# First MoE: the last 1024 tokens take layer one as seven products, and attention ends within two chunks

## The chip, the cores and the metric

The program runs on one core of a Trainium2 chip. The time is the device time of one execution in microseconds (us); the median of three runs of the kernel before is 2063.89 us (2061.16 to 2064.94).

## The reference, cut to what matters

Three stages follow each other. Attention with a window of 128 over 4 x 576 tokens, 8 heads of 64, gives x (2304 x 512). A first MoE layer with one expert gives g = relu(x w_in)^2 (2304 x 2048) and x2 = g w_out. A second one has eight experts that all tokens pass, weighted by a matrix that 16 alternating normalisations (the Sinkhorn loop) make from x2 w_gate.

```python
def _moe_ref(x, w_in, w_out):        # 2304 x 512, 512 x 2048, 2048 x 512
    h = x @ w_in
    r = np.maximum(h, 0.0)
    g = r * r
    return (g @ w_out).astype(np.float32)
```

## The kernel before, in words

Every fp32 product is made of two parts: a value is split into a high part (rounded by ScalarE, L113 or L117) and a low part (the difference, by GpSimd at L114 or VectorE at L114 and L118), and mm3 (L122 to L124) issues three matmuls: high by high, high by low, low by high.

The first MoE goes through the tokens in five chunks: 256 tokens (chunk 0, plain fp32 with narrowed weights), then four of 512 (chunks 1 to 4). In a chunk the 2048 columns of w_in go by in 16 steps f of 128. A step has layer one (gemm1, twelve matmuls of 512 columns into the PSUM tile h), the rectifier on ScalarE (L827), the square on VectorE (L830), the split of the square into gh and gl, and layer two of the step two before (moe1_tail, twelve matmuls into the four PSUM tiles acc). h has one PSUM buffer in chunks 0 to 3; in chunk 4 it takes the three banks that attention used (L822). Split weights are loaded from DRAM in each chunk (a from d_in, b from d_out); in chunk 1 they are split first (L113, L114). A chunk's result is split out of acc (moe1_finish), added up by GpSimd and stored to d_x2 (keep), and its gate logits come from gate_sums and gate_logits.

Attention is a list of small steps. part(i) is called three times in each f of chunks 0 to 3 and issues so many of them that the tokens of chunk c+1 are done when chunk c ends; put_x splits an attention output into xh and xl of its chunk. At the start of chunk 4 the attention pools are closed, load_q(0) loads the second MoE's first token operands, and x_op forms its seven sums and splits. After chunk 4 the slab of the second MoE's first unit is made (raw_w1, sums_w1, split_w1).

The second MoE uses Strassen's scheme in Winograd's form already: seven products for a 2 x 2 block product (GP lists the weight operand, the token operand and the PSUM bank). Its loops are not touched but for the banks of its unit 0.

Until the end of chunk 4 a scheduler orders each engine's instructions; from L859 on each engine runs in the order of the code. Each engine's queue is in order throughout.

Of the kernel before, what the change touches and what calls it, by code (L numbers as in the profile page):

```python
# [8 lines left out]
F32 = mybir.dt.float32  # L9
# [20 lines left out]
def attention_moe_moe2(  # L30
# [32 lines left out]
    NTT = NT // P  # L63

# [19 lines left out]
    xh, xl = [], []  # L84
# [18 lines left out]
    for c in range(3):  # L103
        new_x(xp, c)

# [315 lines left out]
    def put_x(ps, hp, t0, n):  # L421
        o = 0
        while o < n:
# [7 lines left out]
            split_ps(ps[:, o : o + w], xh[c][:, hp, at : at + w], xl[c][:, hp, at : at + w])  # L431
# [110 lines left out]

    words = {}
# [80 lines left out]
    def gate_sums(c):  # L624
        n = chunk(c)[1]
        lp, tag = (ps_at, "at") if c < NCH - 1 else (ps_mm, "mm")
# [17 lines left out]
    def gate_logits():  # L644
# [5 lines left out]
        lp = ps_at.tile([P, 512], F32, name="lp", tag="at")  # L650
# [122 lines left out]
    LAG = 2  # L773
    pending, sums = [], []
    turns = [(c, f) for c in range(NCH) for f in range(NF1)]
# [12 lines left out]
    for c in range(NCH):  # L788
        c0, n = chunk(c)
        if c == 1:  # L790
# [6 lines left out]
            xp2 = m1.enter_context(tc.tile_pool(name="xp2", bufs=1))  # L797
            for i in range(3, NCH):
                new_x(xp2, i)

        advance(needed(c0 + n))
        if c == NCH - 1:
            att.close()
            p2 = ctx.enter_context(tc.tile_pool(name="p2", bufs=1, side="right"))
            p3s = ExitStack()
            p3 = p3s.enter_context(tc.tile_pool(name="p3a", bufs=1, side="right"))
            load_q(0)
            for nm, eng in (("b11", 0), ("b21", 1), ("t1", 0), ("t2", 1), ("t3", 0), ("t4", 1), ("b22", 0)):
                x_op(nm, (nc.vector, nc.gpsimd)[eng])
        for f in range(NF1):  # L810
            now[:] = c, f
            a, bw = ahead.pop(0)
# [9 lines left out]
            hp, tag = (ps_mm, "mm") if c < NCH - 1 else (ps_at, "at")  # L822
            ph = hp.tile([P, 512], F32, name="h1", tag=tag)
# [28 lines left out]
    raw_w1(0)  # L852
    raw_w1(1)
    for x in range(2):
        sums_w1(0, x)
    for x in range(2):
        split_w1(0, x)

    ctx.enter_context(tc.manual_schedule())  # L859

# [63 lines left out]
    def g_product(n, p):  # L924
        o, b, bk = GP[p]
        first = p in (0, 1, 3)
        if first:
            gb[bk] = g_bank(f"g{bk}")
# [218 lines left out]

    moe1_tail(*pending[0])
    moe1_tail(*pending[1])
    moe1_finish(pending[1][0], pending[1][2])  # L1150
    pp = None
    for n in range(NP):
        if n == 0:
# [274 lines left out]
```

## Time and profile before

| | us |
|---|---|
| median of three runs | 2063.89 |
| span of the profiled execution (the only time that it has of its own) | 2061.8 |
| attention's start, until the first layer-one matmul of chunk 0 | 33 |
| chunk 0 with attention | 109 |
| chunks 1 to 3 with attention | 358 |
| chunk 4 | 88 |
| second MoE | 1474 |

The profile is of one execution. The page gives each engine's busy share; the window rows give the same for a stretch, with the granted clock of TensorE (1.00 is 2.4 GHz) and what the DMA engines moved; the timeline gives single instructions with start and duration. A matmul's duration overlaps with the next one's, so the time of a run of matmuls is read from their starts. A duration on VectorE or GpSimd includes the time for which the instruction was held back after its issue.

### The profile page before, as it was taken

What the parts mean: (1) busy time and instruction counts of PE and PEld (TensorE: products, weight loads), DVE (VectorE), ACT (ScalarE), POOL (GpSimd) and SP (SyncE); (2) the same over time, 40 slices, a digit from 0 to 9 for tenths busy, and PEclk for the clock granted to TensorE, in tenths of its full rate; (3) what the DMA queues carried; (4) which work ended last, traced back from release to release, by engine and by line L of the source; (5) the groups of instructions that cost most, each with busy time, mean ns of one, the idle gap of its engine ahead of it and who ended that gap; (6) DMA issues with size and microseconds to landing.
All of it is one profiled execution on the core that took longest, in us unless ns stands there. A gap on an engine that the chain in (4) does not pass through costs nothing.

```text
span 2061.8 us, 31510 instructions
## 1 busy us (share of the span) xinstructions
PE 2025.9 (98%) x10869; PEld 1854.1 (90%) x10869; DVE 1385.8 (67%) x2469; ACT 955.5 (46%) x1950; POOL 1080.9 (52%) x836
## 2 busy tenths in 40 slices
PE   7989999999999999999999999999999999999999
PEld 5767777887888899999999999999999999999999
DVE  7986755535147887777786766776676577667765
ACT  7665655434244444444444434444444444444443
POOL 4224343434358788788785444544454454445442
PEclk9999999999999999999999999999999999999999
DMA  7877877656649878887879878777786787877773
GB/s 208 280 211 252 265 221 195 193 164 204 209 159 327 295 307 319 320 310 287 313 297 343 285 254 256 259 259 256 253 273 228 260 256 260 258 256 235 270 260 106
DMA packets 290653, 523.84 MB, mean 254 GB/s; under 512 B 90416, under 2 KB 135104, under 8 KB 286400
## 3 DMA queue, kind: packets, MB, share of 16 engines
q1 hardware_dynamic: 290496, 521.85, 75.9%
q8 instruction: 87, 1.43, 0.3%
q14 instruction: 70, 0.57, 0.1%
HBM read 369.12 MB, written 152.64 MB: 253 GB/s over the span
## 4 chain that ended last, share of the span: by engine, by line
PE 69%; DVE 4%; issue 1%; ACT 1%; POOL 1%; DMA 0%; ACTq 0%; POOLq 0%; DVEq 0%
PE y L123 11%; PE y L124 11%; PE y L122 11%; PE g L122 11%; PE g L124 11%; PE g L123 11%; PE acc L122 1%; PE acc L123 1%; PE acc L124 1%; PE h L123 1%; PE h L122 1%; PE h L124 1%; DVE s L737 1%; DVE s L739 0%; DVE o L1044 0%
## 5 line engine op out<-in xcount | busy, mean ns | idle before, releaser
L1236 POOL TENSOR_TENSOR rb<-R,rb 128x768 fp32r<-128x768 f32 x95 | 214.0, 2253 | 345.3 <-ACT rb L1231 321.6
L1272 DVE TENSOR_TENSOR a<-y,a 128x384 f32<-128x384 f32 x420 | 232.4, 554 | 192.5 <-PE y L124 192.5
L1236 POOL TENSOR_TENSOR rt<-R,rt 128x768 fp32r<-128x768 f32 x121 | 230.4, 1915 | 138.5 <-ACT rt L1231 59.4
L114 POOL TENSOR_TENSOR w2a<-r,w2a 128x1024 fp32r<-128x1024 f32 x64 | 154.2, 2410 | 66.9 <-ACT w2a L113 66.9
L122 PE MATMUL g<-xt,w1o 128*128 128x384 f32 x512 | 173.8, 339 | 1.4 <-ACT u L947 1.0
L124 PE MATMUL g<-xt,w1o 128*128 128x384 f32 x512 | 172.6, 337 | 0.0
L123 PE MATMUL g<-xt,w1o 128*128 128x384 f32 x512 | 172.3, 337 | 0.0
L122 PE MATMUL y<-rt,w2o 128*128 128x384 f32 x496 | 168.1, 339 | 0.1
L123 PE MATMUL y<-rt,w2o 128*128 128x384 f32 x496 | 168.0, 339 | 0.0
L124 PE MATMUL y<-rt,w2o 128*128 128x384 f32 x496 | 167.4, 337 | 0.0
L1231 ACT ACTIVATE rt<-R 128x768 fp32r<-128x768 f32 x122 | 102.7, 842 | 134.7 <-DVE R L1217 84.0
L114 POOL TENSOR_TENSOR gl<-r,gh 128x512 fp32r<-128x512 f32 x64 | 83.0, 1297 | 155.9 <-ACT gh L113 130.9
L124 PE MATMUL y<-w2a,rl 128*128 128x512 f32 x384 | 150.1, 391 | 0.0
L123 PE MATMUL y<-w2a,rh 128*128 128x512 f32 x384 | 149.6, 390 | 0.2 <-POOL w2a L114 0.2
L122 PE MATMUL y<-w2a,rh 128*128 128x512 f32 x384 | 149.5, 389 | 0.0
L1212 DVE TENSOR_TENSOR R<-R,pb 128x768 f32<-128x768 f32 x128 | 138.5, 1083 | 5.4 <-ACT R L1338 3.9
L122 PE MATMUL y<-rb,w2o 128*128 128x384 f32 x408 | 138.3, 339 | 0.6 <-DVE a L1272 0.6
L123 PE MATMUL y<-rb,w2o 128*128 128x384 f32 x408 | 138.3, 339 | 0.0
L124 PE MATMUL y<-rb,w2o 128*128 128x384 f32 x408 | 137.6, 337 | 0.0
L122 PE MATMUL g<-xb,w1o 128*128 128x384 f32 x384 | 129.9, 338 | 0.0
L124 PE MATMUL g<-xb,w1o 128*128 128x384 f32 x384 | 129.5, 337 | 0.0
L123 PE MATMUL g<-xb,w1o 128*128 128x384 f32 x384 | 129.3, 337 | 0.0
(261 smaller groups left out, 5773.2 us busy)
## 6 DMA issues: line engine op xcount, KB each, us to landing
w1o<-d_w SPq DMA_DIRECT2D x448, 256.0 KB, 3.0
w2o<-d_w SPq DMA_DIRECT2D x218, 512.0 KB, 3.9
d_w<-w1a SPq DMA_DIRECT2D x32, 1792.0 KB, 11.6
d_w<-w2a SPq DMA_DIRECT2D x30, 1536.0 KB, 7.9
r<-in_moe_w_dram SPq DMA_DIRECT2D x64, 512.0 KB, 4.3
a<-d_in SPq DMA_DIRECT2D x48, 512.0 KB, 3.8
b<-d_out SPq DMA_DIRECT2D x48, 512.0 KB, 3.9
u<-in_moe_w_in_dram SPq DMA_DIRECT2D x16, 512.0 KB, 5.0
```

Of the source, the lines that this page charges most:

```text
L114: (eng or nc.gpsimd).tensor_sub(lo, src, raw(hi))
L122: nc.tensor.matmul(ps, lhsT=lh, rhs=rh, start=first, stop=False, **kw)
L123: nc.tensor.matmul(ps, lhsT=lh, rhs=rl, start=False, stop=False, **kw)
L124: nc.tensor.matmul(ps, lhsT=ll, rhs=rh, start=False, stop=last, **kw)
L737: nc.vector.tensor_sub(w1s[n][:, 2], w1s[n][:, 1], a11)
L1212: nc.vector.tensor_mul(r, r, pb[:, None, :].to_broadcast([P, 2, HALF]))
L1231: nc.scalar.activation(x[:, 0], R[m, f, h], AF.Copy)
L1236: eng.tensor_sub(x[:, 1], R[m, f, h], raw(x[:, 0]))
L1272: nc.vector.tensor_add(acc[dst][:, dt], ps[:, :HALF], acc[dst][:, dt])
```

## The change

Chunks 1 and 2 stay as they are. Chunks 3 and 4 (1024 tokens) become one block with two token halves t. Attention writes their x unsplit (xr, by ScalarE alone) and ends four steps before the end of chunk 2; in these four steps early_super splits the seven token operands (b11, b21, t1 to t4, b22: two quarters of K by 512 tokens each, 128x1024) and makes the first weight slab. Layer one then runs as eight units u of two steps f. A unit has seven products of six matmuls of 512 columns; its raw weights come from d_w, and the slab of the next unit is summed (super_sums) and split (super_split) beside it. The squares go to DRAM (d_g), as whole fp32. Four PSUM banks are used in turn, so that product 0 of the next unit stands between products 4 and 5. Layer two follows as 32 steps j, first the 16 of token half 0, then those of half 1; w and g are loaded five steps ahead and g is split two steps ahead. The second MoE's x_op, raw_w1, sums_w1 and split_w1 are spread over the steps of layer two. The diff's core:

```diff
+    PLAIN_CH = NCH - 2
...
     def part(i):
         c, f = now
-        if c < NCH - 1:
-            a, b = [needed(starts[x] + widths[x]) for x in (c, c + 1)]
+        if c == 0:
+            a, b = [needed(starts[x] + widths[x]) for x in (0, 1)]
             advance(a + (b - a) * (3 * f + i) // (3 * NF1))
+        else:
+            a, b = needed(starts[2]), len(steps)
+            advance(min(b, a + (b - a) * (3 * (f + (c - 1) * NF1) + i) // (3 * ((PLAIN_CH - 1) * NF1 - CALM))))
...
+    def early_super(at):
+        if at == 0:
+            advance(len(steps))
+            att.close()
+            sp = sps.enter_context(tc.tile_pool(name="sp", bufs=1, side="right"))
+            super_raw(0)
+            super_raw(1)
+            super_x("b11", 0)
+            super_x("b21", 1)
+        elif at == 1:
+            super_sums(0, False)
+            super_sums(0, True)
+            super_split(0, False)
+            super_x("t1", 0)
+        elif at == 2:
+            super_split(0, True)
+            super_x("t2", 0)
+            super_x("t3", 1)
+        else:
+            super_raw(2)
+            super_x("t4", 0)
+            super_x("b22", 1)
...
+            if c == PLAIN_CH - 1 and f >= NF1 - CALM:
+                early_super(f - NF1 + CALM)
...
-            hp, tag = (ps_mm, "mm") if c < NCH - 1 else (ps_at, "at")
-            ph = hp.tile([P, 512], F32, name="h1", tag=tag)
+            ph = ps_mm.tile([P, 512], F32, name="h1", tag="mm")
...
+    def s_evict(u, p):
+        v1, v3, v2 = s_banks(u)
+        if p == 0:
+            nc.scalar.copy(s_temp("m1"), v1)
+        elif p == 1:
+            super_split(u + 1, False)
+            nc.vector.tensor_add(v3, v3, stemps["m1"])
+            s_square(u, v3, 0, 0)
+        elif p == 2:
+            nc.scalar.copy(s_temp("u2"), v1)
+            super_sums(u + 1, False)
+        elif p == 3:
+            super_sums(u + 1, True)
+        elif p == 4:
+            nc.scalar.copy(s_temp("u3"), v1)
+            super_split(u + 1, True)
+            nc.vector.tensor_add(v3, v2, stemps["u3"])
+            s_square(u, v3, 1, 1)
+        elif p == 5:
+            super_raw(u + 3)
+            s_square(u, v1, 1, 0)
+        elif p == 6:
+            nc.vector.tensor_add(v2, v2, stemps["u2"])
+            s_square(u, v2, 0, 1)
...
+    slots = [(0, 0)]
+    for u in range(NU):
+        slots += [(u, 1), (u, 2), (u, 3), (u, 4), (u + 1, 0), (u, 5), (u, 6)]
+    moe1_tail(*pending[0])
+    for u, p in slots:
+        if u == NU:
+            b_product(0, (0, 1))
+            b_load(4)
+            continue
+        s_product(u, p)
+        if (u, p) == (0, 0):
+            moe1_tail(*pending[1])
+        s_evict(u, p)
...
+    X_AT = {4: ("b11", 0), 5: ("b21", 1), 6: ("t1", 0), 7: ("t2", 1), 8: ("t3", 0), 9: ("t4", 1), 10: ("b22", 0)}
+    for j in range(2 * NF1):
+        if j:
+            b_product(j, range(NK))
+        b_load(j + 5)
+        b_split(j + 2)
+        if j in X_AT:
+            nm, eng = X_AT[j]
+            x_op(nm, (nc.vector, nc.gpsimd)[eng])
```

In super_x and x_op, t1 to t4 each begin with a subtraction on VectorE in place; the number behind the name says which engine makes the low part, 0 for VectorE and 1 for GpSimd.

**The burst of splits on VectorE.** Before, at the start of chunk 4: q are the second MoE's token quarters, xb and xt its operands, h_5995 the layer-one result of f = 0, acc the finished chunk 3.

```order
L830 SCALAR_TENSOR_TENSOR r<-h_5959,r 128x512
L114 TENSOR_TENSOR xb_5930<-q,xb_5930 128x768
L703 TENSOR_TENSOR q<-q 128x768
L707 TENSOR_TENSOR q<-q 128x768
L114 TENSOR_TENSOR xt_5937<-q,xt_5937 128x768
L114 TENSOR_TENSOR xb_5952<-q,xb_5952 128x768
L705 TENSOR_TENSOR q<-q 128x768
L114 TENSOR_TENSOR xt_5945<-q,xt_5945 128x768
L709 TENSOR_TENSOR q<-q 128x768
L830 SCALAR_TENSOR_TENSOR r<-h_5995,r 128x512
L118 TENSOR_TENSOR xl_2008<-acc_5081,xh_2007 128x512
```

With the change, in the last four steps of chunk 2: xr are the unsplit token quarters, sb and st the operands (5147 is b11, 5198 t1), ss the weight sums, h_5157 and h_5205 the results of f = 12 and 13.

```order
L118 TENSOR_TENSOR sb_5147<-xr_2015,sb_5147 128x1024
L810 TENSOR_TENSOR xr_2015<-xr_2016,xr_2015 128x1024
L917 SCALAR_TENSOR_TENSOR r<-h_5157,r 128x512
L839 TENSOR_TENSOR ss<-sr 128x256
L843 TENSOR_TENSOR ss<-sr 128x256
L840 TENSOR_TENSOR ss<-ss,sr 128x256
L814 TENSOR_TENSOR xr_2016<-xr_2016 128x1024
L842 TENSOR_TENSOR ss<-sr,ss 128x256
L118 TENSOR_TENSOR st_5198<-xr_2015,st_5198 128x1024
L812 TENSOR_TENSOR xr_2015<-xr_2016,xr_2015 128x1024
L917 SCALAR_TENSOR_TENSOR r<-h_5205,r 128x512
L816 TENSOR_TENSOR xr_2015<-xr_2015 128x1024
```

A burst of the same kind moves from chunk 4 into chunk 2, with pieces of 1024 columns for 768, and squares stand inside it. On GpSimd the same place reads, before and with the change:

```order
L114 TENSOR_TENSOR gl<-r,gh 128x512
L114 TENSOR_TENSOR xb_5933<-q,xb_5933 128x768
L114 TENSOR_TENSOR xt_5941<-q,xt_5941 128x768
L114 TENSOR_TENSOR xt_5949<-q,xt_5949 128x768
L114 TENSOR_TENSOR gl<-r,gh 128x512
```

```order
L118 TENSOR_TENSOR sb_5150<-xr_2015,sb_5150 128x1024
L118 TENSOR_TENSOR sb_5291<-xr_2016,sb_5291 128x1024
L118 TENSOR_TENSOR sw<-sr,sw 128x6x128
L118 TENSOR_TENSOR gl<-r,gh 128x512
L118 TENSOR_TENSOR st_5244<-xr_2016,st_5244 128x1024
L118 TENSOR_TENSOR sw<-ss,sw 128x8x128
```

Three splits of 768 become five of 768 to 1024 (sb_5150 is b21, sb_5291 b22, st_5244 t3, sw the slab).

**TensorE at the next layer-one product.** Before, in chunk 4, from layer two of the step before into layer one of f = 1, with what each waits for in brackets:

```order
L122 MATMUL acc_5093<-gh,b 128x512
L123 MATMUL acc_5093<-gl,b 128x512
L124 MATMUL acc_5093<-gh,b 128x512
L122 MATMUL h_6039<-xh_2009,a 128x512 [waits DMAHW0_49,PE_49]
L123 MATMUL h_6039<-xl_2010,a 128x512
```

With the change, in chunk 2, into layer one of f = 13:

```order
L126 MATMUL acc_4148<-gh,b 128x512
L127 MATMUL acc_4148<-gl,b 128x512
L128 MATMUL acc_4148<-gh,b 128x512
L126 MATMUL h_5205<-xh_93,a 128x512 [waits DMAHW6_49,DVE_49]
L127 MATMUL h_5205<-xl_94,a 128x512
```

The first matmul of h waits for VectorE here, since the square of the step before reads the same bank.

**VectorE through one unit.** In chunk 4 of before VectorE had one square for each step and nothing else; with the change a unit reads as follows (s1 to s3 are the PSUM banks, sm1, su2 and su3 ScalarE's copies, gs the squares, ss the sums for the next unit):

```order
L979 TENSOR_TENSOR s1_5333<-s1_5333,sm1_5891 128x512
L970 SCALAR_TENSOR_TENSOR gs_5928<-s1_5333,r_5926 128x512
L839 TENSOR_TENSOR ss_5939<-sr_5814 128x256
L840 TENSOR_TENSOR ss_5939<-ss_5939,sr_5814 128x256
L842 TENSOR_TENSOR ss_5939<-sr_5814,ss_5939 128x256
L843 TENSOR_TENSOR ss_5939<-sr_5814 128x256
L989 TENSOR_TENSOR s1_5333<-s2_5334,su3_5956 128x512
L970 SCALAR_TENSOR_TENSOR gs_5963<-s1_5333,r_5961 128x512
L970 SCALAR_TENSOR_TENSOR gs_5986<-s0_5332,r_5984 128x512
L995 TENSOR_TENSOR s2_5334<-s2_5334,su2_5937 128x512
L970 SCALAR_TENSOR_TENSOR gs_5998<-s2_5334,r_5996 128x512
```

Two squares of a pair of steps become four squares, three additions and four sums for 42 layer-one matmuls.

## Rows read from the trace of the kernel before

**Rows 1.** The page, busy us of each engine (share of the span) x instructions.
```profile
PE 2025.9 (98%) x10869; PEld 1854.1 (90%) x10869; DVE 1385.8 (67%) x2469; ACT 955.5 (46%) x1950; POOL 1080.9 (52%) x836
```
**Rows 2.** Timeline of PE in chunk 4: start, duration (us), line, names, shapes.
```profile
560.78 0.39 PE L122 MATMUL h<-xh,a 128*128 128x512 f32 x1
...
563.50 0.39 PE L122 MATMUL acc<-gh,b 128*128 128x512 f32 x1
...
579.59 0.39 PE L124 MATMUL h<-xh,a 128*128 128x512 f32 x1
```
**Rows 3.** Windows of chunk 0: length, busy us (x count), clock, DMA share, GB/s.
```profile
33.00:142.00 109.00, 103.49 (x561) 80.14 (x560) 99.63 (x285) 73.33 (x217) 22.09 (x38) 0.98 0.81 245
```
**Rows 4.** Windows of chunks 1 to 3 (PE, PEld, DVE, ACT, POOL).
```profile
142.00:202.00 60.00, 57.44 (x306) 44.56 (x306) 41.76 (x129) 37.27 (x101) 27.05 (x45) 1.00 0.75 245
202.00:262.00 60.00, 58.35 (x312) 45.68 (x310) 41.06 (x130) 38.32 (x106) 21.25 (x33) 1.00 0.84 270
262.00:382.00 120.00, 119.40 (x653) 95.14 (x652) 66.34 (x237) 61.36 (x182) 44.84 (x76) 1.00 0.72 202
382.00:500.00 118.00, 117.88 (x592) 94.34 (x591) 46.73 (x135) 45.26 (x113) 40.79 (x57) 1.00 0.60 187
```
**Rows 5.** Timeline of PE where chunk 4 begins, idle before in brackets.
```profile
502.27 0.39 PE L629 MATMUL lt<-xh,wgs 128*72 128x512 f32 x1
504.95 0.50 PE L122 MATMUL acc<-gh,b 128*128 128x512 f32 x1 [2.29 <-DVE xl L118]
505.29 0.40 PE L123 MATMUL acc<-gl,b 128*128 128x512 f32 x1
...
507.44 0.63 PE L123 MATMUL acc<-gl,b 128*128 128x512 f32 x1
507.87 0.63 PE L124 MATMUL acc<-gh,b 128*128 128x512 f32 x1
```
**Rows 6.** Windows where chunk 4 begins and in the second MoE.
```profile
502.00:510.00 8.00, 5.71 (x18) 4.01 (x18) 8.00 (x10) 4.70 (x9) 7.01 (x5) 0.79 0.31 108
800.00:850.00 50.00, 50.00 (x252) 45.33 (x251) 38.18 (x55) 23.68 (x39) 42.60 (x33) 1.00 0.92 355
```
**Rows 7.** Timeline of DVE: subtractions, a square, sums of the second MoE.
```profile
496.86 2.50 DVE L707 TENSOR_TENSOR q<-q 128x768 f32<-128x768 f32 x1
...
501.01 0.94 DVE L705 TENSOR_TENSOR q<-q 128x768 f32<-128x768 f32 x1
...
580.71 0.69 DVE L830 SCALAR_TENSOR_TENSOR r<-h,r 128x512 f32<-128x512 f32 x1 [4.75 <-ACT r L827]
...
621.72 0.42 DVE L736 TENSOR_TENSOR s<-r 128x256 f32<-128x256 f32 x1
622.17 2.51 DVE L737 TENSOR_TENSOR s<-s,r 128x256 f32<-128x256 f32 x1
```
**Rows 8.** Timeline of POOL beside them.
```profile
495.97 2.57 POOL L114 TENSOR_TENSOR xb<-q,xb 128x768 fp32r<-128x768 f32 x1
...
507.13 1.30 POOL L114 TENSOR_TENSOR gl<-r,gh 128x512 fp32r<-128x512 f32 x1
...
613.00 2.41 POOL L114 TENSOR_TENSOR w1a<-s,w1a 128x1024 fp32r<-128x1024 f32 x1
...
621.83 2.56 POOL L114 TENSOR_TENSOR w2a<-r,w2a 128x1024 fp32r<-128x1024 f32 x1 [1.17 <-ACT w2a L113]
```
**Rows 9.** Timeline of ACT: a split of 1024 and a rectifier.
```profile
512.48 1.06 ACT L113 ACTIVATE w1a<-s 128x1024 fp32r<-128x1024 f32 x1 [4.53 <-DVE s L739]
...
580.08 0.60 ACT L827 ACTIVATE r<-h 128x512 f32<-128x512 f32 x1 [3.45 <-PE h L124]
```

More of the change, by code (lines that the diff above doesn't have):

```diff
@@ L82, in chunk @@
         return starts[c], widths[c]
-    xh, xl = [], []
+    xh, xl, xr = [], [], []
     def new_x(pool, c):
@@ L541, in narrow @@
         nc.vector.tensor_add(w, t[2], t[3])
+    d_g = [dram.tile([P, 2, 2, CH], F32, name=f"d_g{u}") for u in range(NF1 // 2)]
     words = {}
@@ L787, in attention_moe_moe2, with super_x @@
     qstack = []
-    for c in range(NCH):
+    xr_stack = ExitStack()
+    sps = ExitStack()
+    sx, sr, ss, sslab = {}, {}, {}, {}
+    NU = NF1 // 2
+    def super_x(nm, eng):
+        q = {(h, t): xr[t][:, 2 * h : 2 * h + 2] for h in range(2) for t in range(2)}
+        if nm == "t1":
+            nc.vector.tensor_sub(q[0, 0], q[0, 1], q[0, 0])
+        elif nm == "t2":
+            nc.vector.tensor_sub(q[0, 0], q[1, 1], q[0, 0])
+        elif nm == "t3":
+            nc.vector.tensor_sub(q[0, 1], q[1, 1], q[0, 1])
+        elif nm == "t4":
+            nc.vector.tensor_sub(q[1, 0], q[1, 0], q[0, 0])
+        at = {"b11": (0, 0), "t1": (0, 0), "t2": (0, 0), "b21": (1, 0), "t4": (1, 0), "t3": (0, 1), "b22": (1, 1)}[nm]
+        x = sx[nm] = sp.tile([P, 2, 2, CH], F32R, name=f"s{nm}")
+        split_sb(q[at], x[:, 0], x[:, 1], (nc.vector, nc.gpsimd)[eng])
@@ L789, in attention_moe_moe2 @@
+    sp = None
+    for c in range(PLAIN_CH):
         c0, n = chunk(c)
@@ L796, in attention_moe_moe2 @@
                     nc.gpsimd.memset(raw(x), 0.0)
-            xp2 = m1.enter_context(tc.tile_pool(name="xp2", bufs=1))
-            for i in range(3, NCH):
-                new_x(xp2, i)
+            xp2 = xr_stack.enter_context(tc.tile_pool(name="xp2", bufs=1))
+            for i in range(PLAIN_CH, NCH):
+                xr.append(xp2.tile([P, NK, CH], F32, name=f"xr{i}"))
         advance(needed(c0 + n))
[L802 to L809, printed above, removed]
         for f in range(NF1):
             now[:] = c, f
+            if c == PLAIN_CH - 1 and f >= NF1 - CALM:
+                early_super(f - NF1 + CALM)
             a, bw = ahead.pop(0)
@@ new lines, in attention_moe_moe2, with b_product @@
+    baccs = []
+    def b_product(j, ds):
+        h, f = divmod(j, NF1)
+        (w, _), (gh, gl) = btiles[j], bparts[j]
+        for d in ds:
+            if f == 0 and h == 0:
+                baccs.append(ps_acc.tile([P, 512], F32, name=f"acc{d}", tag="acc"))
+            acc1 = sbank[d] if h else baccs[d]
+            col = slice(d * P, (d + 1) * P)
+            mm3(acc1, (w[:, 0, col], w[:, 1, col]), (gh, gl), f == 0, f == NF1 - 1)
+            if f == NF1 - 1:
+                finish_part(PLAIN_CH + h, d, acc1)
```

143 lines of the change are left out of this document (128 added, 15 removed).

## The prediction

> **What bounds the kernel now.** I read the page first, then busy time by stage, then what TensorE waited for, then the timelines of the stages that the change touches. TensorE is busy 98% of the span [rows 1], so a change pays by taking matmuls away, and it costs whatever TensorE then has to wait. A 512-column matmul of the first MoE starts every 0.227 us: twelve of them lie between 560.78 and 563.50 [rows 2]. The window rows give what the other engines let through by stage. In chunk 0 TensorE is idle 5.5 of 109 us with VectorE 91% busy [rows 3]. In chunks 1 to 3 it is idle 2.6 of 60 us at a VectorE share of 70%, 1.7 of 60 at 68%, 0.6 of 120 at 55%, 0.1 of 118 at 40% [rows 4]. Where chunk 4 begins there is one hole of some size: a matmul starts at 502.27, the next at 504.95, and then the matmuls are 0.43 us apart, at the lower of the two clock levels (1.2 GHz) [rows 5]. Between 502 and 510 only 18 start, where 35 fit, at a granted clock of 0.79 [rows 6]: 17 x 0.227 = 3.9 us lost.
>
> **What the change takes away.** Layer one of chunks 3 and 4 took 2 x 16 x 12 = 384 matmuls of 512 columns. Seven products of six matmuls for eight units are 336. 48 x 0.227 = **-10.9 us**. Layer two keeps its 384. The hole at the start of chunk 4 came from the second MoE's operand splits, put there together with the end of chunk 3. They now stand one to a step of layer two, so I take the whole hole off: **-4.0 us**.
>
> **The new burst ahead of the Strassen products.** In the last four steps of chunk 2 (f = 12 to 15) VectorE gets, beside its four squares, four subtractions and four low parts of 1024 columns and four sums of 256. GpSimd gets three low parts of 1024, the first slab's 768 and 1024, and the usual low parts of g. What this costs hangs on how the two engines stand each other. A 768-column subtraction on VectorE takes 0.94 us alone (501.01), and 2.50 us (496.86 to 499.36) beside a GpSimd split that ran from 495.97 to 498.54. A 256-column sum takes 0.42 alone (621.72), and 2.51 (622.17 to 624.68) beside a split that ended at 624.39 [rows 7, 8]. In both, VectorE's end is GpSimd's end plus a rest under 1 us: the instructions go one after the other, and by turns where both have work queued. The Trainium skill, SBUF — State Buffer, section "Who interferes with whom", states this as a rule that speaks against the change: a VectorE instruction with two SBUF inputs and a GpSimd instruction that reads SBUF share a port pair, and the one that comes later is blocked until the other is done. The two pairs of rows agree with it. The rows could also be read as two engines that share a rate (0.94 stretched to 2.50, 2.41 to 3.3); worked through in that way, the holes below come to 10 us, by the rule to the 11.6 of the hand schedule, and the bounds hold both.
>
> Why that reaches TensorE: in chunk 2 the layer-one result h has one PSUM buffer, so the matmuls of f+1 wait until VectorE has squared f, and between the two stand only twelve layer-two matmuls, 2.72 us. In chunk 4 of before h had three buffers. VectorE's queue is in order, and between the square of 12 and that of 13 stand seven instructions of the burst.
>
> By hand, from the first matmul of h(12), t = 0: ScalarE copies the last attention tile and makes three high parts of 1.06 [rows 9] before the rectifier of 12, done at 4.5. VectorE: low part b11 1.85 to 3.1 (1024 columns alone: 0.94 and 0.42 give 1.04 ns a column, so 1.21). GpSimd: low part b21 (2.41 [rows 8]) 3.1 to 5.5. VectorE: t1 5.5 to 6.7, square of 12 to 7.4. h(13) could have started at 5.44 and starts at 7.45: **2.0 us**. Then by turns: GpSimd b22 to 9.05, a sum to 9.5, GpSimd slab 768 (1.8: 2.57 less its wait, 495.97) to 11.3, a sum, GpSimd g(12) (1.3) to 13.0, a sum to 13.4, t3 to 14.6, the last sum to 15.05, low t1 to 16.3, GpSimd t3 to 18.65, t2 to 19.9, square of 13 to 20.6. h(14) was due at 7.45 + 5.44 = 12.9 and starts at 20.65: **7.75**. Then t4, low t2 and low t4, between GpSimd's slab sums and g(13), to 27.2, square of 14 to 27.9: h(15) due at 26.1, starts at 27.95: **1.85**. Sum 11.6. Ends: if nothing takes turns, VectorE's work between two squares is 4 x 0.42 + 3 x 1.21 + 0.69 = 6.0 against 5.44, a stall of about 1; if turns fall worse, 15. The idle of 2.3 us at 502 was followed by a stretch at 1.2 GHz that cost eight matmuls 0.2 us each, 1.6 us [rows 5]; here most of such a stretch falls into time that h(15) waits anyway, so I add 0.8 (0 to 3.2, two such stretches). **+12.4 us**, 1 to 18.
>
> **The Strassen products.** Each unit has one tight loop. From the end of product 6 of the unit before: result visible (579.59 + 0.23 to 580.08, so 0.27 [rows 2, 9]), VectorE's add 0.69, rectifier 0.60, square 0.69 (580.71 [rows 7]), the next add 0.69, rectifier 0.60, copy 0.60, with six hand-overs of 0.03 to 0.05: 4.4 us. Only then may product 4 write the bank that the copy reads; products 1 to 3 cover 3 x 1.36 = 4.08. So 0.3, and 0.1 because the first matmul after a wait runs at a wider spacing (504.95 to 505.29, 0.34 for 0.23 [rows 5]): 0.4 x 7 units = 2.9. In units 1 and 2 four extra GpSimd additions for the layer's output fall beside VectorE's sums, and ScalarE's slab split waits for these: 0.6 each, 1.3 in all. **+4.2 us**, 1 to 8.
>
> **Attention in two chunks.** Its work on every engine stays but is spread over 28 steps instead of 48, some 250 us instead of 358. VectorE's share in chunk 1 rises from about 69% to some 75%. TensorE's idle share at 68 to 70% is 2.8 to 4.3%, at 91% it is 5.1% [rows 3, 4]. Taking 4% of chunk 1's new 142 us and 0.9% of chunk 2's remaining 107 gives 6.7, against 4.9 now: **+1.8 us**. Ends: -2 (the output copies of 1024 tokens lose VectorE's low part) and +8 (5.1% all along).
>
> **Layer two behind, and the joins.** Each step of 2.72 us loads 512 + 256 KB, 289 GB/s; a stretch of the second MoE moved 355 GB/s while TensorE had no gap [rows 6]. Loads are five steps ahead, so I cost them nothing; without that cover each step that is late adds its lateness. GpSimd has one low part of g (1.3) and in every other step of 4 to 10 a 768 split, plus turns with VectorE: 7.2 us in two steps of 5.4, a backlog of about 3 us against a lead of 5.4. The first two steps of layer two read squares that went through DRAM a few us before. **+1.0 us**, 0 to 5. The start of the second MoE keeps its order and I cost it nothing.
>
> **Sum.** -10.9 - 4.0 + 12.4 + 4.2 + 1.8 + 1.0 = +4.5 us: the span of 2061.8 becomes 2066.3. The profiled execution's span lies 2.1 us under the median of the three runs, 2063.89; with that on top, 2068.4. A measurement of this kernel can tell about 0.2%, 4.1 us, from no change.
>
> **Rivals.** *The turns don't reach TensorE.* If VectorE gets through f = 12 to 14 in 6 us a step (VectorE's instructions served first, or GpSimd idle at the time), the burst costs 1 and the Strassen loop 3: -14.9 + 1 + 3 + 1.5 + 1 = -8.4, **2055.5**. For it: the sums alone take 0.42, and some rows show them so. Against: both engines' queues are full there. It decides at 5.4 us of VectorE time between two squares. *Half of it.* Turns fall better and the burst costs 6: -1.9, **2062**. *Attention becomes VectorE-bound.* If chunks 1 and 2 idle like chunk 0, 5.1% of 250 us is 12.7 for 4.9: +7.8 in place of +1.8, **2074.4**. For it: chunk 0's rows. Against: chunk 0's VectorE also narrows the weights, and from 55% to 70% of VectorE the idle share of TensorE rises by 2 to 4 points only [rows 4].
>
> **How the numbers follow.** The forecast, 2068.4, gets 0.44 (its own range 2063 to 2073, from the ends of the four costs taken half way); the free burst 0.22, half the burst 0.20, attention 0.14. The range reaches from the free burst to a little over the attention case: 2055 to 2077. Slower by over 0.2%, that is over 2068: half of the forecast and the attention case, 0.38; faster: the free burst and a tail of the half, 0.25; within: the rest, 0.37.
>
> **What would show it.** Each step right: the matmuls of the first MoE are 48 fewer at the same 0.227 us; three holes before h(13), h(14), h(15), the middle one the longest, each ended by VectorE's square, with sums and low parts there that take their own time plus a GpSimd instruction's; a hole of about 0.4 us before product 4 of each unit, ended by ScalarE's copy; no hole in layer two over 1 us; TensorE idle in the attention stretch 3 to 5%. Wrong: squares that end within 5.4 us of each other, or holes in chunk 1 of over 8 us in all, or TensorE waiting for DMA in layer two.

## The result and the profile after

The changed kernel takes 2077.71 us (median of 4 runs, 2076.28 to 2079.27), the kernel before 2064.41 in the same session: a ratio of 1.0065 with a 95% interval of 1.0051 to 1.0080. It is slower, by 13.3 us, where 4.5 were forecast; the time lies 0.7 us above the range. The profiled span went from 2061.8 to 2075.5, by 13.7.

The page's line of the engines (busy us, share of the span, instructions), the answer to [rows 1] (PE is TensorE, PEld its weight loads, DVE VectorE, ACT ScalarE, POOL GpSimd; SP, further down, is the engine that issues the transfers):

```profile
PE 2022.5 (97%) x10821; PEld 1844.5 (89%) x10821; DVE 1430.1 (69%) x2513; ACT 985.9 (48%) x1997; POOL 1127.0 (54%) x855
```

TensorE has the 48 matmuls fewer that the change promised, and the span is longer all the same: what was won is lost in waits. Where, the windows of after show (length, busy us of PE, PEld, DVE, ACT and POOL with their counts, granted clock, DMA share, GB/s), the answer to [rows 4, 6]:

```profile
142.00:202.00 60.00, 56.62 (x318) 42.51 (x317) 45.14 (x142) 38.76 (x110) 26.60 (x49) 1.00 0.74 240
202.00:262.00 60.00, 58.61 (x321) 44.71 (x320) 44.51 (x161) 40.50 (x125) 23.07 (x42) 1.00 0.74 223
380.00:410.00 30.00, 22.77 (x95) 17.97 (x94) 23.77 (x16) 13.11 (x17) 18.54 (x8) 0.89 0.38 119
410.00:492.00 82.00, 81.17 (x355) 64.78 (x354) 49.61 (x83) 42.75 (x71) 36.20 (x19) 1.00 0.40 133
492.00:505.00 13.00, 9.13 (x31) 6.52 (x30) 3.21 (x6) 4.01 (x7) 2.54 (x2) 0.87 0.88 294
505.00:600.00 95.00, 90.51 (x393) 72.21 (x392) 20.43 (x22) 30.72 (x50) 57.61 (x41) 1.00 0.82 277
```

Two stretches stand out by their clock of 0.89 and 0.87: the burst (380 to 410) and the place where the products end and layer two begins (492 to 505). The Strassen products themselves (410 to 492) run nearly without a gap.

To set the terms side by side I take times between marks of the trace, because chunk 0 ends some 3 us sooner or later from one run to the next: the first layer-one matmul of chunk 1 (141.5 us here), that of step 12 of chunk 2 (380.4), the first product (414.4), the first g matmul of the second MoE (600.3). Work is counted in matmuls at the 0.227 us of [rows 2].

| term | forecast | measured in the trace of after |
|---|---|---|
| 48 matmuls fewer | -10.9 | -10.9 (10869 - 10821, spacing unchanged) |
| hole at chunk 4's start | -4.0 | -4.8 (99.5 us from chunk 4 on, 94.7 of them work) |
| burst ahead of the products | +12.4 | +9.6 (34.1 us from step 12 to the first product, 24.5 of them work) |
| Strassen products, to 492 us | +4.2 | +2.6 |
| attention in two chunks | +1.8 | +3.0 (238.8 us to step 12; before, less its 20 further steps, 235.8) |
| joins (492 to 505) and layer two | +1.0 | +6.3 and +6.7 |
| second MoE | 0 | +1.4 (600.3 to the end, 1475.2 us; before 1473.8) |
| sum | +4.5 | +13.9 (the spans: +13.7; chunk 1 starts 0.2 us sooner in after) |

One line carries the miss: the joins and layer two, 13.0 for 1.0. A hole, here and below, is a wait of TensorE, counted from matmul start to matmul start less the usual 0.227 us; half clock means its lower level, 1.2 GHz, at which the matmuls stand 0.43 us apart.

**The burst.** VectorE and then GpSimd, in the timeline of after (start, duration, line, names, shapes, idle before):

```profile
381.99 1.23 DVE L118 TENSOR_TENSOR sb<-xr,sb 128x1024 fp32r<-128x1024 f32 x1 [3.59 <-DMA b<-d_out]
383.25 3.32 DVE L810 TENSOR_TENSOR xr<-xr,xr 128x1024 f32<-128x1024 f32 x1
386.49 0.68 DVE L917 SCALAR_TENSOR_TENSOR r<-h,r 128x512 f32<-128x512 f32 x1
387.09 2.02 DVE L839 TENSOR_TENSOR ss<-sr 128x256 f32<-128x256 f32 x1
389.03 2.06 DVE L843 TENSOR_TENSOR ss<-sr 128x256 f32<-128x256 f32 x1
391.01 1.51 DVE L840 TENSOR_TENSOR ss<-ss,sr 128x256 f32<-128x256 f32 x1
392.44 1.21 DVE L814 TENSOR_TENSOR xr<-xr 128x1024 f32<-128x1024 f32 x1
393.58 0.41 DVE L842 TENSOR_TENSOR ss<-sr,ss 128x256 f32<-128x256 f32 x1
...
395.16 3.25 DVE L812 TENSOR_TENSOR xr<-xr,xr 128x1024 f32<-128x1024 f32 x1
398.33 0.68 DVE L917 SCALAR_TENSOR_TENSOR r<-h,r 128x512 f32<-128x512 f32 x1
```

```profile
383.04 5.78 POOL L118 TENSOR_TENSOR sb<-xr,sb 128x1024 fp32r<-128x1024 f32 x2 [3.24 <-ACT sb L117]
388.78 2.03 POOL L118 TENSOR_TENSOR sw<-sr,sw 128x768 fp32r<-128x768 f32 x1
390.76 1.48 POOL L118 TENSOR_TENSOR gl<-r,gh 128x512 fp32r<-128x512 f32 x1
```

A 256-column sum takes 0.41 us alone (393.58) and 2.02 beside a GpSimd split; a 1024-column subtraction 1.21 alone and 3.32 beside one. Each of the three long sums ends 0.3 us after a GpSimd instruction does (388.82, 390.81, 392.24), as worked out by hand: a constant rest speaks for turns, and against two engines that share a rate. The square of step 13 ends 18.7 us after h(12) starts (forecast 20.6), and it ends the longest hole of the stretch. The timeline of PE there:

```profile
392.57 0.39 PE L128 MATMUL acc<-gh,b 128*128 128x512 f32 x1
399.07 0.79 PE L126 MATMUL h<-xh,a 128*128 128x512 f32 x1 [6.11 <-DVE r L917]
399.66 0.63 PE L127 MATMUL h<-xl,a 128*128 128x512 f32 x1
```

**The join.** ScalarE, PE and SP's queue of transfers around 497 us, in the timeline of after:

```profile
494.81 0.63 ACT L117 ACTIVATE gh<-gq 128x512 fp32r<-128x512 f32 x1 [0.80 <-DMA gq<-d_g]
500.11 0.63 ACT L117 ACTIVATE gh<-gq 128x512 fp32r<-128x512 f32 x1 [4.67 <-DMA gq<-d_g]
500.65 0.57 ACT L987 COPY su<-s 128x512 f32<-128x512 f32 x1
```

```profile
497.87 0.39 PE L128 MATMUL acc<-gh,w 128*128 128x512 f32 x1
501.27 0.58 PE L126 MATMUL s<-st,sw 128*128 128x512 f32 x1 [3.02 <-ACT su L987]
501.64 0.63 PE L127 MATMUL s<-st,sw 128*128 128x512 f32 x1
502.07 0.63 PE L128 MATMUL s<-st,sw 128*128 128x512 f32 x1
```

```profile
491.68 2.92 SPq L971 DMA_DIRECT2D d_g<-gs  x3
494.65 0.42 SPq L1006 DMA_DIRECT2D w<-d_out  x1
495.12 0.44 SPq L1008 DMA_DIRECT2D gq<-d_g  x1
```

Product 5 of the last unit needs a bank that ScalarE's copy su (L987) reads. That copy stands in ScalarE's queue behind the high part of the second g (500.11), which waits 4.67 us for a transfer; and the load of that g was issued at 495.12 only, behind three stores of squares that wait for VectorE. Behind the wait of 3.2 us the matmuls stand 0.43 us apart for 3 us, at half clock. Ahead of it, at 497 us, TensorE waits 1.0 us for GpSimd's low part of the first g.

**Layer two.** TensorE waits four more times between 523 and 536 us (1.10, 1.12, 0.90, 0.88 us) and once at 585 (1.40). The first and the fourth of these in the timeline of PE, and the windows of that stretch:

```profile
523.29 0.39 PE L128 MATMUL acc<-gh,w 128*128 128x512 f32 x1
524.62 0.50 PE L126 MATMUL acc<-gh,w 128*128 128x512 f32 x1 [0.94 <-ACT gh L117]
...
536.18 0.50 PE L127 MATMUL acc<-gl,w 128*128 128x512 f32 x1 [0.72 <-POOL gl L118]
```

```profile
515.00:525.00 10.00, 9.06 (x39) 6.88 (x38) 2.00 (x2) 3.18 (x5) 2.95 (x3) 1.00 1.03 405
525.00:535.00 10.00, 8.41 (x36) 6.56 (x36) 6.75 (x5) 5.04 (x8) 10.00 (x6) 1.00 1.03 397
```

Two suspects stand in these rows. The DMA engines are busy all the time, at 405 and 397 GB/s; and in the second window GpSimd, which makes the low parts of g, is busy 10.0 of 10 us. In the timelines of ScalarE and GpSimd ahead of the fourth wait, operands of the second MoE stand in front of g:

```profile
530.52 0.85 ACT L117 ACTIVATE xt<-q 128x768 fp32r<-128x768 f32 x1 [2.03 <-DVE q L714]
531.27 0.62 ACT L117 ACTIVATE gh<-gq 128x512 fp32r<-128x512 f32 x1
```

```profile
531.60 2.57 POOL L118 TENSOR_TENSOR xt<-q,xt 128x768 fp32r<-128x768 f32 x1
534.12 3.97 POOL L118 TENSOR_TENSOR gl<-gq,gh 128x512 fp32r<-128x512 f32 x2
```

That g had landed at 529.71 us, 6.5 us before TensorE could go on. And SP shows that the loads aren't five steps ahead: from 514 to 526 us each of its twelve issues of w and g comes at most 0.07 us after the eighth transfer before it has landed (514.37 after 514.30, 516.07 after 516.01). In the whole execution no more than eight transfers are under way at once, which is four steps of w and g. Whether more of them would have helped at 405 GB/s, no run shows.

### The profile page after: what moved, and what is told of

Same layout as the page of the kernel before. It is cut to its first block, busy times and chain, and to the rows that moved or that the text cites. A ratio compares the mean times of both kernels' runs of the same rounds, so it can differ in the third digit from the quotient of the medians.

```text
span 2075.5 us, 31718 instructions
## 1 busy us (share of the span) xinstructions
PE 2022.5 (97%) x10821; PEld 1844.5 (89%) x10821; DVE 1430.1 (69%) x2513; ACT 985.9 (48%) x1997; POOL 1127.0 (54%) x855
## 4 chain that ended last, share of the span: by engine, by line
PE 80%; DVE 6%; DMA 3%; ACT 2%; POOL 2%; issue 2%; SPq 0%; ACTq 0%; POOLq 0%; DVEq 0%
PE y L127 11%; PE y L128 11%; PE y L126 11%; PE g L126 10%; PE g L128 10%; PE g L127 10%; PE acc L127 1%; PE acc L128 1%; PE s L126 1%; PE s L127 1%; PE s L128 1%; PE acc L126 1%; PE h L126 1%; PE h L128 1%; PE h L127 1%
## 5 line engine op out<-in xcount | busy, mean ns | idle before, releaser
L1572 ACT ACTIVATE R<-u 128x384 f32<-128x384 f32 x128 | 67.3, 526 | 127.6 <-DVE u L1192 86.4
```

Of the source, the lines that this page charges most:

```text
L1572: nc.scalar.activation(R[m, f, h][:, pair], src, AF.Relu)
```

## Experiments

Medians of different sessions are compared through their ratio to the kernel before, which ran beside each.

### The burst: banks, turns, and both

In h_banks the layer-one result takes the attention's three PSUM banks where the burst stands:

```diff
-            ph = ps_mm.tile([P, 512], F32, name="h1", tag="mm")
+            hp, tag = (ps_at, "at") if c == PLAIN_CH - 1 and f >= NF1 - CALM else (ps_mm, "mm")
+            ph = hp.tile([P, 512], F32, name="h1", tag=tag)
```

> The changed kernel, but in the last four steps of chunk 2 h takes the three PSUM banks that attention has left, so that layer one of f+1 doesn't wait for the square of f. Theory 1 (the burst costs TensorE time only through the one h bank): the holes before h(13) and h(14) and the half-clock stretch go, 9.3 us: about 2068.5. Theory 2 (VectorE's burst is late for everything, and the wait moves on to layer two of f = 12, which needs g(12) and g(13), or to the first products): half of it comes back as waits for the low part of g, about 2073.

2072.44 us, ratio 1.0043 (1.0031 to 1.0056), as theory 2 has it. The waits for VectorE's square are gone and step 14 starts at 391.1 us instead of 399.1, but only 3.8 of the 9.6 us stay won at the first product. The rest comes back behind, before the second matrix's matmuls, where GpSimd's low part of g is late; the timeline of PE in h_banks:

```profile
399.92 0.50 PE L126 MATMUL acc<-gh,b 128*128 128x512 f32 x1 [0.47 <-ACT gh L117]
402.77 0.50 PE L127 MATMUL acc<-gl,b 128*128 128x512 f32 x1 [2.34 <-POOL gl L118]
```

In all_vector GpSimd's three low parts of operands in the burst (b21, t3, b22) go to VectorE, which is the fuller engine:

```diff
-            super_x("b21", 1)
+            super_x("b21", 0)
...
-            super_x("t3", 1)
+            super_x("t3", 0)
...
-            super_x("b22", 1)
+            super_x("b22", 0)
```

> The changed kernel, but the low parts of b21, b22 and t3 (128x1024) are made by VectorE instead of GpSimd: VectorE has three instructions more in the burst, GpSimd three fewer. If VectorE is late because it takes turns with GpSimd, the sums and subtractions between the squares of f = 12 and 13 lose most of their waits (11.2 us down to 7 to 9) and the hole before h(14) shrinks from 6.3 to 2 to 4 us. If VectorE simply has too much work there, the stretch stays at 11 us or grows by up to 3.6, and the hole with it.

2070.83 us, ratio 1.0038 (1.0024 to 1.0052). VectorE has three more instructions of 1024 columns and is done sooner: in the 30 us from step 12 on it is busy 21.26 us, where the 30 us from 380 in after hold 23.77. The hole before h(14) falls from 6.3 to 1.9 us, another of 2.5 stands before h(15), no half clock follows, and chunk 1's start to the first product takes 268.4 us instead of 272.9. So GpSimd's instructions had held VectorE up; a shared rate would explain that as well as turns. For turns speaks the rest of 0.3 us again: the two sums that still fall beside GpSimd take 1.48 and 1.51 us and end at 385.10 and 386.53, GpSimd's instructions at 384.81 and 386.24.

vector_banks has both edits.

> all_vector and h_banks together: in the last four steps of chunk 2 VectorE takes the low parts of b21, t3 and b22 too, and h takes the attention's four banks. all_vector left holes of 4.4 us that VectorE's square ends (h's one bank), h_banks left 3.3 us that GpSimd's low part of g ends. If each of them leaves what the other takes away, the stretch has under 1.5 us of holes and no half clock, and the median is 2066.5 to 2069. If VectorE is simply too full in these four steps (the squares and the low parts of g then come late whatever banks there are), 3 us or more of holes remain, now before the second matrix's matmuls, and the median is 2070 to 2072.5.

2067.65 us, ratio 1.0022 (1.0012 to 1.0031); to the first product 264.9 us, 8.0 less than in after. One hole of 1.3 us is left, with no half clock. Each edit takes away what the other leaves. The timeline of VectorE in vector_banks shows two of the same sums, the first still beside GpSimd's split of the slab (until 385.19), the second beside its low part of g (until 386.63):

```profile
384.00 1.48 DVE L839 TENSOR_TENSOR ss<-sr 128x256 f32<-128x256 f32 x1
385.40 1.51 DVE L843 TENSOR_TENSOR ss<-sr 128x256 f32<-128x256 f32 x1
```

### The join: the loads' place, then ScalarE's order

early_loads issues the first four loads of w and g one unit earlier:

```diff
-        elif u == NU - 1 and p < 4:
-            b_load(p)
-            if p > 1:
-                b_split(p - 2)
+        elif u == NU - 2 and p in (1, 2, 3, 4):
+            b_load(p - 1)
+        elif u == NU - 1 and p in (2, 3):
+            b_split(p - 2)
```

> The changed kernel, but the weights and squares of layer two's first four steps are loaded during unit 6 instead of unit 7. If the 5.8 us that TensorE loses around the end of the products come from the queue's order (the loads stand behind stores that wait for VectorE, the split of g waits for its load in ScalarE's queue, and the copy that frees a bank stands behind it), the split of g(0) and g(1) finds its data, the 3.2 us wait for the copy and the 1.0 us wait for the low part go, with the half clock: about 2072, and later steps gain a little. If the transfers are late because the DMA engines are full there, the loads land late all the same and under 2 us come back.

2074.41 us, ratio 1.0050 (1.0036 to 1.0064); from the first product to the second MoE 182.7 us instead of 185.9. The g loads are there in time and no half clock follows, but 2.4 of the 3.2 us of the hole stay. The timeline of ScalarE in early_loads says why:

```profile
494.95 0.64 ACT L117 ACTIVATE gh<-gq 128x512 fp32r<-128x512 f32 x1
499.54 0.63 ACT L117 ACTIVATE gh<-gq 128x512 fp32r<-128x512 f32 x1 [3.94 <-DMA d_g<-gs]
500.07 0.57 ACT L987 COPY su<-s 128x512 f32<-128x512 f32 x1
```

The second split no longer waits for its load but for a store: gh shares its three buffers with the squares gs, and this one is still on its way to DRAM.

split_late is early_loads with the second split behind the copies:

```diff
-        elif u == NU - 1 and p in (2, 3):
-            b_split(p - 2)
+        elif u == NU - 1 and p in (2, 5):
+            b_split(p // 5)
```

> The four first loads of layer two stand one unit earlier, as in early_loads, and besides ScalarE's split of the second g stands behind the bank copies of the last unit. In early_loads the hole behind the first two steps of layer two stayed (2.42 us at 498.05), released by a bank copy of ScalarE that came behind the split of the second g. Theory A (ScalarE works in order, and a copy that TensorE needs stands behind a split that waits for a transfer): that hole falls to under 0.5 us and the half clock behind it goes, the second MoE starts 3 to 5 us sooner than in early_loads, the median is 2069 to 2071.5. Theory B (VectorE's additions or the banks set the hole, ScalarE's wait only shows beside it): the hole stays at 2 us or over, the median is 2073.5 to 2075.

2070.58 us, ratio 1.0038 (1.0025 to 1.0051); 180.3 us to the second MoE. The timeline of ScalarE in split_late:

```profile
493.25 0.59 ACT L987 COPY su<-s 128x512 f32<-128x512 f32 x1 [1.24 <-PE s L128]
...
497.16 0.63 ACT L117 ACTIVATE gh<-gq 128x512 fp32r<-128x512 f32 x1 [0.21 <-DMA d_g<-gs]
```

The copy now waits for TensorE alone, and between 485 and 505 us TensorE is busy 20.00 of 20 us. So the hole was ScalarE's order: a copy that TensorE needs behind a split that nobody needs yet.

### Layer two: transfers or GpSimd

w_half loads the weights for every second step alone, and the step between multiplies by those of the step before (half of w is left out):

```diff
-            w = mp.tile([P, 2, DM], F32R, name="w", tag=("b", "a")[j % 2], bufs=(4, 3)[j % 2])
-            nc.sync.dma_start(raw(w), d_out[f])
+            if j % 2 == 0:
+                b_load.w = mp.tile([P, 2, DM], F32R, name="w", tag=("b", "a")[j // 2 % 2], bufs=(4, 3)[j // 2 % 2])
+                nc.sync.dma_start(raw(b_load.w), d_out[f])
+            w = b_load.w
```

> In layer two of the last two halves the weights are loaded for every second step alone, the step between them multiplies by those of the step before: half of the weights are left out, so what is computed is not the reference's, every instruction of the engines but 16 loads of 512 KB remains. From 515 to 535 us the trace of after has the DMA engines busy 1.03 of the time at 397 to 405 GB/s, with g landing 7.7 us after its issue. Theory A (the transfers are at their limit there and bring g late): the holes before layer two's matmuls at 523 to 536 us (4.0 us) fall under 1.5 us, and g lands in under 5 us; the median is 2072 to 2074.5. Theory B (GpSimd sets them, whose low parts of g stand behind its halves of the seven operands): the holes stay at 3 us or over, the median is 2076.5 to 2078.

2073.41 us, ratio 1.0053 (1.0037 to 1.0070). The holes of 523 to 536 us fall from 4.0 to 1.0 us; the hole of the join falls to 1.7. Between 515 and 537 us g lands 5.3 us after its issue in the median, where it took 7.7 and theory A asked for under 5; but the loads of g issued up to 519.3 us still take 6.8 us and more, since the DMA engines are full until 525 here too. They were issued sooner: the g that lands at 523.83 us in after lands at 517.15. The two windows in w_half, GpSimd in the second as full as in after:

```profile
515.00:525.00 10.00, 10.00 (x44) 7.97 (x43) 5.79 (x5) 4.37 (x7) 7.03 (x5) 1.00 1.03 396
525.00:535.00 10.00, 9.31 (x41) 7.26 (x40) 6.01 (x4) 4.36 (x7) 10.00 (x6) 1.00 0.75 240
```

x_vector is the counterpart: the three low parts that GpSimd makes for the second MoE in layer two go to VectorE, the transfers stay.

```diff
-    X_AT = {4: ("b11", 0), 5: ("b21", 1), 6: ("t1", 0), 7: ("t2", 1), 8: ("t3", 0), 9: ("t4", 1), 10: ("b22", 0)}
+    X_AT = {4: ("b11", 0), 5: ("b21", 0), 6: ("t1", 0), 7: ("t2", 0), 8: ("t3", 0), 9: ("t4", 0), 10: ("b22", 0)}
```

> The three of the seven operands of the second MoE whose low part GpSimd takes in layer two (b21, t2, t4) go to VectorE, so that GpSimd has the low parts of g alone; the transfers stay as they are. It is the counterpart of w_half. Theory A (transfers late): ScalarE's and TensorE's waits for g stay, the holes at 523 to 536 us stay at 2.5 us or over, the median is 2076 to 2078. Theory B (GpSimd late): the holes fall under 1.5 us, the median is 2074 to 2075.5.

2076.92 us, ratio 1.0068 (1.0053 to 1.0083). GpSimd's time falls to 4.10 us in the same window, and TensorE is busy no longer:

```profile
525.00:535.00 10.00, 8.37 (x29) 6.25 (x28) 6.31 (x5) 4.28 (x7) 4.10 (x3) 0.83 1.04 393
```

The holes to 536 us come to 2.1 us, a little under what the theory of transfers asked and well over the other's 1.5; two more, 1.8 us, stand at 540 and 544, and the clock falls to 0.83. So neither suspect has it all. The first two of after's four holes (2.2 us) stand here too and are gone in w_half, with GpSimd at 10.0 of 10 us: they are the transfers'. The fourth is left in w_half (0.85 us) and gone here: it was the operands of the second MoE that stood ahead of g on ScalarE and GpSimd. The third is gone in both, so it seems to have needed both a late g and GpSimd's half of an operand ahead of its low part. The two new holes are of the fourth's kind: ScalarE's high part of g stands behind the split of an operand that waits 2.5 us for VectorE, which has more to do now.

### Everything together, and the same mending for the kernel before

joined is vector_banks with split_late's edits.

> vector_banks and split_late together. The two edits act on stretches that follow each other: in vector_banks the first Strassen product starts at 404.4 us (414.4 in after), in split_late the second MoE starts 180.3 us after the first product (185.9 in after). If each gain is kept, the second MoE starts at 585 us, 15.6 us sooner than in after, and the median is 2061 to 2064, the time of before. If one of them is given back (the burst's gain by loads that are then late, or the join's by the transfers), 2065 to 2068.

2062.39 us, ratio 0.9994 (0.9985 to 1.0003): the gains add up (265.5 us to the first product, 179.8 from there to the second MoE), and the time is that of before.

joined_later moves the second MoE's preparation within layer two:

```diff
-        if j == 1:
+        if j == 6:
             load_q(0)
...
-    X_AT = {4: ("b11", 0), 5: ("b21", 1), 6: ("t1", 0), 7: ("t2", 1), 8: ("t3", 0), 9: ("t4", 1), 10: ("b22", 0)}
+    X_AT = {9: ("b11", 0), 10: ("b21", 1), 11: ("t1", 0), 12: ("t2", 1), 13: ("t3", 0), 14: ("t4", 1), 15: ("b22", 0)}
...
-        elif j == 11:
-            raw_w1(0)
-            raw_w1(1)
-        elif j in (20, 21):
-            sums_w1(0, j == 21)
-        elif j in (22, 24):
-            split_w1(0, j == 24)
+        elif j in (16, 17):
+            sums_w1(0, j == 17)
...
+        if j == 10:
+            raw_w1(0)
+        elif j == 12:
+            raw_w1(1)
+        elif j in (18, 20):
+            split_w1(0, j == 20)
```

> joined, and in layer two the four loads of the second MoE's operands stand at step 6 instead of 1, their splits at steps 9 to 15 instead of 4 to 10, and the work on its first weights at steps 16 to 20 instead of 20 to 24, ahead of the stores of x that GpSimd makes from step 21 on. Theory A (layer two's holes come from transfers that meet at its start, and at 585 us from GpSimd's queue): of the 5.3 us of holes in split_late (515.2 to 527, and 1.40 at 577) under 1.5 us remain, the median is 2057 to 2060.5, under before. Theory B (the weights alone, 768 KB a step, are too much for the transfers): the holes move to the later steps, 3 us or more remain, and the median is 2061 to 2064.

2059.16 us (11 runs, 2058.45 to 2060.32), ratio 0.9979 (0.9970 to 0.9988): faster than both kernels. Two holes of 0.85 us are left in layer two, 1.7 in all where under 1.5 were expected, and from the first product to the second MoE it takes 176.2 us, 9.7 less than in after. The windows of its start in joined_later:

```profile
507.00:517.00 10.00, 10.00 (x45) 8.28 (x45) 0.00 (x0) 2.78 (x6) 5.17 (x4) 1.00 1.03 390
517.00:527.00 10.00, 10.00 (x46) 8.26 (x44) 4.73 (x4) 4.10 (x6) 6.33 (x5) 1.00 1.04 396
```

The DMA engines are as full as in after. What changed is whose bytes are in the way: the 1.5 MB of load_q now come when w and g are some steps ahead. The operands' splits moved with them, so this run doesn't tell the two causes apart.

before_spread gives the kernel before the same kind of mending: the seven operands of the second MoE are made one by one in steps 4 to 10 of chunk 4, not all at its start.

```diff
-            load_q(0)
-            for nm, eng in (("b11", 0), ("b21", 1), ("t1", 0), ("t2", 1), ("t3", 0), ("t4", 1), ("b22", 0)):
-                x_op(nm, (nc.vector, nc.gpsimd)[eng])
...
+            if c == NCH - 1 and f == 1:
+                load_q(0)
+            elif c == NCH - 1 and f in X_AT:
+                nm, eng = X_AT[f]
+                with tc.issue_after(rl.ins), tc.issue_after(sq.ins):
+                    x_op(nm, (nc.vector, nc.gpsimd)[eng])
```

> The kernel before, with the seven operands of the second MoE's first block made one by one in steps 4 to 10 of its last chunk instead of all at that chunk's start. Its hole at 502 us, with the half clock behind it, comes to 4.8 us. Theory A (the hole is the operands' burst on VectorE, ahead of the low parts of x): the hole falls under 1 us, the median is 2058 to 2060, as low as joined_later's 2059.2; what joined_later has over before is then not the seven products', but mending that before takes as well. Theory B (the low parts of x come late by themselves): the hole stays at 3 us or over, the median is 2062.5 to 2064.

2059.12 us, ratio 0.9977 (0.9968 to 0.9986). The hole is gone; where chunk 4 begins, PE in before_spread goes straight on, for [rows 5]:

```profile
502.27 0.39 PE L122 MATMUL acc<-gh,b 128*128 128x512 f32 x1
502.50 0.39 PE L123 MATMUL acc<-gl,b 128*128 128x512 f32 x1
```

So the 4.4 us that joined_later has over before are to be had without the seven products: mended alike, the two forms take the same time. What eats the 10.9 us of the 48 matmuls even then, by the trace of joined_later: 3.1 us in attention (238.9 us to step 12), 1.7 in the burst (26.1 us, 24.5 of them work) and 5.9 from the first product to the second MoE (176.2 us, 170.3 of them work).

### Attention in two chunks

att_two is the kernel before with attention issued within chunks 1 and 2; att_two_spread the same on before_spread:

```diff
-        if c < NCH - 1:
-            a, b = [needed(starts[x] + widths[x]) for x in (c, c + 1)]
+        if c == 0:
+            a, b = [needed(starts[x] + widths[x]) for x in (0, 1)]
             advance(a + (b - a) * (3 * f + i) // (3 * NF1))
+        elif c < NCH - 1:
+            a, b = needed(starts[2]), len(steps)
+            advance(min(b, a + (b - a) * (3 * (f + (c - 1) * NF1) + i) // (3 * (2 * NF1 - 4))))
```

> The kernel before, with one part of the change alone: all attention steps are issued within chunks 1 and 2 (by four steps before the end of chunk 2); chunk 3 runs without attention. From the traces the part of TensorE's time that isn't first-MoE matmuls grew by 2.6 us; the prediction said +1.8, with -2 to +8. Expected +1 to +4 us over the kernel before. If the close spacing is what costs most of the 13.3 us, +6 and more.

2073.22 us, ratio 1.0047 (1.0035 to 1.0060), 9.5 us over the kernel before where 1 to 4 were expected. The run doesn't measure attention alone: with attention over, the second MoE's operands were scheduled into the last steps of chunk 2 (not chunk 3, as the next expectation says), where h has one bank. The holes before its steps 14 and 15, at 393 and 404 us, and the half clock behind come to 8.9 us against before's 4.8.

> before_spread, and attention's steps within chunks 1 and 2 alone, as the change issues them. In att_two, the same on before itself, the operands' burst came into chunk 3 and hid the price. What this kernel has over before_spread is the price of attention in two chunks, and nothing else of the change: 1.8 us by the prediction's sum, 3.1 us by the reading of the trace of after from the start of chunk 1 to step 12 of chunk 2 (238.9 us against 235.8), 4.3 us by the same reading of att_two.

2064.20 us against 2059.12: this form of attention in two chunks costs 5.1 us. In the windows from 142 to 382 us TensorE's idle time rises from 4.9 us (before_spread) to 7.3; the first two of these windows in att_two_spread:

```profile
142.00:202.00 60.00, 56.63 (x317) 42.47 (x317) 44.27 (x144) 38.20 (x108) 26.70 (x47) 1.00 0.74 238
202.00:262.00 60.00, 58.17 (x322) 44.10 (x321) 46.00 (x162) 40.53 (x124) 23.27 (x43) 1.00 0.74 225
```

One wait of 0.8 us at 396 us, for VectorE's square, comes on top. The remaining 1.9 us lie in the same waits. A matmul's row is 0.39 us long where the next can start after 0.227, so the windows count up to 0.16 us of every wait as busy, and from chunk 1 to the second MoE att_two_spread has 27 waits to before_spread's 13. Counted from start to start they cost 13.1 us in the one and 7.6 in the other.

The pair is not the change's attention alone, though: in these 28 steps VectorE still makes 19 low parts of attention outputs (6.8 us) that the change leaves out. To step 12 of chunk 2 att_two_spread takes 240.1 us, after 238.8; that is 1.3 us of the difference between 5.1 and 3.0, and the wait at 396 us is 1.0. That the low parts cause the 1.3 us is likely, but no run shows it.

## Why the prediction was wrong

**The step that failed** is "Loads are five steps ahead, so I cost them nothing", the term of layer two and the joins: 1.0 was put there, with 5 as its end, and 13.0 were measured. Three things in it were wrong.

- The first loads were not ahead. They were issued in the last unit, in SP's order behind stores that wait for VectorE's squares. I read the program's step numbers as a lead, without asking what stands in front in SP's queue.
- I looked for the late g at TensorE alone. The split of g stands in ScalarE's queue ahead of a copy that frees a bank for the products, so the late transfer stopped another stage (early_loads against split_late: 2.4 us; the half clock behind had gone with early_loads).
- I compared 289 GB/s of need with 355 GB/s that the second MoE moved without a gap [rows 6], and took the transfers as covered. But a load that starts late has to catch up, at 405 GB/s with every engine busy, and 1.5 MB of the second MoE's x came into just that time. Nor could five steps of w and g be under way: the trace shows eight transfers at most, four steps. The Trainium skill, DMA: Bandwidth & Descriptors, section "Specifications", puts the ceiling of the way into SBUF at 435 GB/s and a core's share of the memory at about 358. The trace's 405 GB/s lies above the second and near the first.

GpSimd's backlog, which I weighed there, was the smaller part: with the operands' splits on ScalarE it made the fourth hole of layer two (0.9 us) and shared in the third (w_half against x_vector). The hole at 585 us is its own: there it has a low part of g and one store addition in every step, and joined_later, which moves the weights' splits ahead of these, cuts it from 1.40 to 0.84 us.

**The burst**, the term that I took for the largest, was right in kind and 2.8 us too dear: +9.6 for +12.4. Place, order of the holes (the second the longest, ended by VectorE's square) and the taking of turns came out; the rivals "free burst" and "half of it" fell. The third hole, 1.85 us, did not come: the square of 14 ended 25.3 us after the start of h(12), not 27.9, and the stretch at half clock took up what was left of the wait. The trace agrees with the rule of the Trainium skill, SBUF — State Buffer, section "Who interferes with whom", that I weighed: five sums of VectorE, in after and all_vector, end 0.3 us after a GpSimd instruction does. In the working, 0.94 and 0.42 us give 1.02 ns a column and not 1.04, which changes nothing: 1.21 us was measured for 1024 columns.

**The Strassen products** came to 2.6 for 4.2. Both of its waits are there, where they were put. Product 4 of units 2 to 7 starts late, by 0.2 us in five of them and by 0.4 in one (at 455 us, ended by ScalarE's copy), where 0.4 was put for each of seven; GpSimd's slab comes late once, by 0.8 us at 446 us, where 1.3 was put. The mechanism was right and the sizes were smaller.

**Attention** cost 3.0 in the trace of after and 5.1 in the pair, which carries more, for 1.8; both lie within its ends of -2 and +8. VectorE's share in chunk 1 is 75% (45.14 of 60 us), as put, and TensorE's idle time in the windows too: 6.1 us from 142 to 380, where I put 6.7. What I missed is that the windows don't show all of what is lost: up to 0.16 us of every wait counts as busy there.

**The hole of before**, -4.0, is confirmed: before_spread gains 4.4 us by it. But it was no merit of the change, as it can be had alone.

**The second MoE**, costed at nothing, is within its scatter: from its first g matmul to the end it takes 1473.8 to 1475.2 us in all traces, of both forms of the kernel.

That the direction came out right is luck: with 1.0 at the joins the measured terms would sum to +1.9, no change that can be told. The slowdown is the joins and layer two.

## What to carry to other kernels

Where one stage feeds the next through DRAM, follow each queue in its own order at the seam: a load's lead begins when SP reaches it, and a split that waits for a load belongs behind every copy that frees a bank. Where VectorE and GpSimd both subtract in SBUF, give all of it to one of them for the time in which TensorE waits for VectorE. And before crediting a rearrangement with a hole that it closes, try whether the old kernel closes it by itself.

## What the runs showed of the hardware

- VectorE was through a burst sooner with three more instructions of 1024 columns (1.21 us each alone), when GpSimd's equal ones, of 2.5 to 2.9 us, no longer came between.
- The 16 DMA engines moved 390 to 405 GB/s over stretches of 10 us. With eight loads of 256 to 512 KB under way, they landed 7.7 to 8.8 us after their issue (after, 514 to 526 us); later, in w_half, at 240 GB/s, g took 3.6 to 5.8.
- Waits of about 1 us left the clock at 2.4 GHz in after (523 to 536 us) and were followed by 0.83 in x_vector; the two longest waits of after, 6.3 and 3.2 us, were each followed by some 3 us at 1.2 GHz. Waits of 2.4 to 2.6 us were followed by it in before (505 us) and h_banks (403 us), and not in early_loads (501 us) and all_vector (399 us).
